# One core, attention then a gated MLP: every engine in written order from the second tile on, with attention's work cut into steps over product slots and the inverse roots folded on partitions

## The chip, the core and the metric

The kernel runs on one core of one Trainium2 chip. The metric is the device time of one execution in microseconds (us), as the median of several runs. The core's engines are TensorE (PE, matmuls), VectorE (DVE), ScalarE (ACT), GpSimd (POOL) and SyncE (SP, which issues most of the DMAs). PE writes its sums to PSUM banks; DVE and ACT read them there.

## The reference

What is computed, cut to what matters:

```python
B, H, S, D = 8, 8, 576, 64                       # q, k, v: fp32
scores = where((rel >= 0) & (rel < 64), q @ k.T / 8, -1e9)   # rel = row - column
attn = exp(scores - max); attn /= sum + 1e-9
x = (attn @ v) as (B*S = 4608 tokens, H*D = 512)
xn = x / sqrt(mean(x*x) + 1e-6) * rms_g
g, val = xn @ w_gate, xn @ w_val                 # 512 x 1536 each
out = (silu(g) * val) @ w_out                    # 1536 x 512
```

## The kernel before

**Tiles.** The 4608 tokens go through the MLP in nine tiles t of 512; the 1536 hidden columns in six chunks c of 256. An fp32 matrix is split in a high and a low half-precision part, and a product is three matmuls (hi·hi, hi·lo, lo·hi; `three`, L799 to L802). Tiles 0 to 2 use ordinary products (`expert_in`: 288 matmuls of 512 columns a tile; gate and value sums `pg`, `pv`). From tile 3 on (`FIRST7 = 3`) `expert_in_7` computes each chunk with seven products in the manner of Strassen: 42 products a tile, each 12 matmuls of 256 columns (L941), in four PSUM banks `bk0`, `bk1`, `bk2`, `bk5`. Between products, ACT copies a bank aside so that it comes free (`snap`, L962: `s1`, `u2`, and `p5`, which lies in `wt11`); DVE adds the copies back (L999, L1002, L1006), and `quad` makes one quarter of a chunk's hidden values: tanh on ACT (L971), two operations on DVE (L972, L973), and for every second one a cast on ACT (L977) and the low part on POOL or, in the last chunk, DVE (L978). `expert_out` then makes the tile's output with 144 matmuls of 512 columns; `store` scales on ACT (L1024, `ot`) and writes by DMA.

**Attention.** Batch b (576 tokens) has four pairs of heads, n = 4b + hp. Batches 0 and 1 are computed up to tile 0 and 1; pairs 8 to 31 beside the MLP, a tile or so ahead of need, in *visits* (`visit`), one every 8 of a tile's 32 half steps. In a visit PE computes the values of pair n − 2 (L511, `xp`) and the scores of pair n (L386, `sc`); then DVE masks and finds minima in nine operations (L399), ACT takes nine exps (L402), DVE finishes the sums (L431, L432); later POOL normalises and moves blocks of 32 rows in sixteen operations (`move`, L371), and DVE transposes 32x32 blocks (`turn`, L374, L375), before visit n + 2. When the fourth pair of a batch has been drained (L573) and squared (L579, L584), `normalise` computes the inverse root mean square: PE sums the squares over partitions and broadcasts them (`tot`, L710), DVE iterates on all 128 partitions (L698, L699, three times L703 to L705: 11 operations, once for each of the two pieces of a batch that fall in two tiles), scales x (L750), and `combine` prepares the seven-product operands (L783 to L796: casts on ACT, low parts on POOL, sums on DVE). In tiles 1 and 2 `prepare` also builds the sums of weights for the seven products (DVE, ACT, DMA) in four steps a chunk.

**What sets the order.** All this is written in one stream: `tick` calls `advance` at half steps, which takes events from a list `plan` sorted by due step. The Tile framework then schedules each engine's queue by its own model of times, within the data's dependences. Only PE is held to the written order, from tile 1, chunk 3 on (`ORDERED = (1, 3)`): `group` issues each group of instructions after PE's last one. DVE, ACT and POOL run their queues in the order that the scheduler gave. An engine takes its queue strictly in order, as the trace shows it: the first instruction that waits holds those behind it.

## Time and profile before

| | us |
|---|---|
| median of 3 runs (1050.73, 1053.23, 1054.05) | 1053.23 |
| the profiled execution | 1047.25 |
| its span, first to last instruction | 1045.5 |
| PE busy | 970.2 |
| DVE busy | 666.3 |
| POOL busy | 529.9 |
| ACT busy | 509.8 |
| mean granted PE clock (1 is full) | 0.974 |

The profile's rows give times from the span's start. In a row of the timeline stand start, duration, engine, line, operation, out<-in and count; in brackets the idle time of the engine ahead of it and the instruction that ended it. In a row of the waits stand who waited for whom, us in total, how often, and the longest. In a row for a stretch of time stand its length, and for each engine the busy time with the number of instructions, then the granted PE clock, the DMA engines' busy share and GB/s.

By the first product of each, the tiles begin at 58.2, 218.9, 337.8, 459.1, 559.5, 664.2, 769.1, 869.6 and 955.7 us, and the last output ends at 1042.0.

### The profile page before, as it was taken

The page shows a single profiled execution, that of the slowest core. Times are in us where ns is not written, and L with a number is a line of the kernel's source. Part 1 is how long each engine was busy: PE and PEld are TensorE (multiplying, and loading weights), DVE is VectorE, ACT ScalarE, POOL GpSimd, SP SyncE. Part 2 cuts the span into 40 slices and gives each one's busy share as a digit, 9 for nine tenths or more (in the row PEclk, how much of TensorE's full clock was granted, in tenths as well). Part 3 has the DMA queues.
Part 4 walks back from the last instruction along what each step waited for, and adds up shares of the span by engine and source line. Part 5 has one row for each costly group of instructions (what it writes and reads, how often), then busy time and mean ns, then how long its engine had stood idle before and what let it go on. Part 6 is the DMA issues. An engine that isn't in the chain of part 4 may idle for free.

```text
span 1045.5 us, 20648 instructions
## 1 busy us (share of the span) xinstructions
PE 970.2 (93%) x7739; PEld 629.6 (60%) x7751; DVE 666.3 (64%) x1725; ACT 509.8 (49%) x1303; POOL 529.9 (51%) x667
## 2 busy tenths in 40 slices
PE   7789987899988799989999899999989999999998
PEld 5444544344444255458846784688568847866875
DVE  5688857447778665856685668666866575531550
ACT  5567877235432444346535663556355524522540
POOL 3425634817856566765765675667566313200210
PEclk9989998999999899999999999999999999999999
DMA  7657963013320554137724672466235514732501
GB/s 284 191 164 218 256 185 92 21 54 117 96 78 26 151 158 146 66 117 232 216 81 148 201 217 85 122 222 219 74 108 176 177 40 141 211 113 78 166 1 41
DMA packets 81316, 143.43 MB, mean 137 GB/s; under 512 B 25792, under 2 KB 38336, under 8 KB 81216
## 3 DMA queue, kind: packets, MB, share of 16 engines
q1 hardware_dynamic: 80640, 140.93, 44.1%
q8 instruction: 61, 1.00, 0.4%
q10 hardware_dynamic: 576, 1.18, 0.3%
q14 instruction: 39, 0.32, 0.1%
HBM read 121.64 MB, written 20.45 MB: 136 GB/s over the span
## 4 chain that ended last, share of the span: by engine, by line
PE 45%; DVE 19%; POOL 18%; ACT 13%; issue 4%; DMA 1%; POOLq 0%; SPq 0%; ACTq 0%; DVEq 0%
POOL pm L371 17%; PE bk L941 16%; ACT pm L402 6%; PE bk L800 3%; PE bk L802 3%; PE bk L801 3%; PE xp L511 3%; DVE xb L750 2%; PE sc L386 2%; DVE pm L374 2%; DVE r L703 2%; PE pg L800 2%; DVE r L704 2%; DVE r L705 2%; PE pg L801 2%
## 5 line engine op out<-in xcount | busy, mean ns | idle before, releaser
L941 PEld LDWEIGHTS <-wt 128*128 128x128 f16 x3024 | 297.5, 99 | 66.4 <-issue 27.6
L371 POOL TENSOR_TENSOR pm<-pm,st 32x288 f32<-32x288 f32 (+1 forms) x384 | 271.6, 707 | 125.2 <-DVE st L432 38.7
L941 PE MATMUL bk<-xn,wt 128*128 128x256 f16 x1728 | 210.3, 274 | 17.4 <-ACT wt L962 7.0
L941 PE MATMUL bk<-wt,wt 128*128 128x256 f16 x1224 | 152.8, 275 | 7.0 <-ACT s L962 7.0
L978 POOL TENSOR_TENSOR h<-th,h 128x512 f16<-128x512 f32 x60 | 69.2, 1158 | 165.7 <-ACT h L977 149.2
L800 PE MATMUL bk<-wt,h 128*128 128x512 f16 (+1 forms) x300 | 111.2, 371 | 0.0
L801 PE MATMUL bk<-wt,h 128*128 128x512 f16 (+1 forms) x300 | 111.1, 370 | 0.0
L802 PE MATMUL bk<-wt,h 128*128 128x512 f16 (+1 forms) x300 | 111.1, 370 | 0.0
L402 ACT ACTIVATE pm<-pm,st 128x128 f32<-128x128 f32 (+1 forms) x216 | 82.1, 381 | 12.8 <-DVE st L399 12.8
L971 ACT ACTIVATE th<-bk,hsc 128x256 f32<-128x256 f32 x108 | 51.1, 473 | 73.1 <-DVE bk L999 37.1
L802 PEld LDWEIGHTS <-h 128*128 128x128 f16 x436 | 42.8, 98 | 53.6 <-issue 5.1
L800 PEld LDWEIGHTS <-h 128*128 128x128 f16 x436 | 43.2, 99 | 49.3 <-issue 3.8
L801 PEld LDWEIGHTS <-h 128*128 128x128 f16 x436 | 42.9, 98 | 47.9 <-issue 2.8
L374 DVE STREAM_TRANSPOSE pm<-pm 128x1024 f32<-128x1024 f32 x24 | 29.8, 1243 | 65.1 <-POOL pm L371 65.1
L972 DVE SCALAR_TENSOR_TENSOR th<-th,bk 128x256 f32<-128x256 f32 x108 | 44.9, 416 | 39.5 <-ACT th L971 39.5
L800 PE MATMUL pg<-xn,wt 128*128 128x512 f16 x144 | 56.8, 394 | 12.0 <-ACT ot L1024 7.9
L386 PE MATMUL sc<-kv,q 64*64 64x128 f32 (+1 forms) x1056 | 57.1, 299 | 8.4 <-DMA q<-q 4.9
L999 DVE TENSOR_TENSOR bk<-bk,s 128x512 f32<-128x512 f32 x36 | 25.1, 696 | 60.7 <-PE bk L941 53.4
L800 PE MATMUL pv<-xn,wt 128*128 128x512 f16 x144 | 56.3, 391 | 7.4 <-DVE th L849 7.3
L801 PEld LDWEIGHTS <-wt 128*128 128x128 f16 x296 | 29.7, 100 | 53.2 <-issue 22.9
L783 ACT CAST xn<-xb 128x192 f16<-128x192 f32 (+7 forms) x33 | 12.9, 423 | 97.1 <-DVE xb L750 97.0
L977 ACT CAST h<-th 128x512 f16<-128x512 f32 x72 | 44.5, 618 | 29.3 <-DVE th L973 29.3
(189 smaller groups left out, 1916.1 us busy)
## 6 DMA issues: line engine op xcount, KB each, us to landing
wt<-sevens SPq DMA_DIRECT2D x108, 512.0 KB, 4.3
kv<-kv SPq DMA_DIRECT2D x28, 608.0 KB, 4.6
wt<-sevens SPq DMA_DIRECT2D x36, 256.0 KB, 3.5
q<-q SPq DMA_DIRECT2D x28, 288.0 KB, 3.6
...
```

Of the source, the lines that this page charges most:

```text
L371: nc.gpsimd.tensor_tensor(m[to, :us, fr], p[fr, :us, to], r, ALU.mult)
L374: nc.vector.transpose(p[:, : NBLK - 1, :], m[:, : NBLK - 1, :])
L386: nc.tensor.matmul(out.rearrange("p (n c) -> p n c", c=D), lhsT=qt[hd, j * D : (j + 1) * D], rhs=halves[hd, :1, :] if j == 0 else halves[h ...
L402: nc.scalar.activation(part, part, AF.Exp, bias=low, scale=-1.0, accum_out=total)
L800: nc.tensor.matmul(acc, lhsT=lh, rhs=rh, start=first, stop=False)
L801: nc.tensor.matmul(acc, lhsT=lh, rhs=rl, start=False, stop=False)
L802: nc.tensor.matmul(acc, lhsT=ll, rhs=rh, start=False, stop=last)
L941: nc.tensor.matmul(acc[:, i * HT : (i + 1) * HT], lhsT=w[:, i, l, kt, :], rhs=b[:, m, kt, :], start=at_start, stop=kt == 1 and j == 2, ski ...
L971: nc.scalar.activation(cols, acc[:, :HT], AF.Tanh, scale=th_scale[:, c : c + 1])
L972: nc.vector.scalar_tensor_tensor(cols, cols, 1.0, acc[:, :HT], ALU.add, ALU.mult)
L977: nc.scalar.copy(hh, th)
L978: (nc.vector if t and c == NC - 1 else nc.gpsimd).tensor_tensor(hl, th, hh, ALU.subtract)
```

## The change

From tile 1, chunk 0 on, `in_written_order` ties each instruction of PE, DVE, ACT and POOL to the one written before it on its engine, so that the scheduler no longer moves any; SP is left free. The code is rewritten so that the written order is meant as it stands. Half steps become halves and fractions; `slot_at` counts in *slots*, one for each product or its like. In a visit, masks are written one to a slot, each exp one slot after its mask, the finish after the last, the sixteen moves one at a time from slot 11.3 on, 0.8 apart, and the transposition as three operations (two of 512 columns for one of 1024, and the rest) from four slots ahead of visit n + 2 on. Tanh and the first gating operation come right after the gate product in tiles 1 and 2; casts and low parts are deferred by one and two slots. Squares come one slot, their sum two slots after the copy.

The inverse roots of a batch (from batch 2 on) are computed once: four matmuls put the sums of 144 tokens each on 32 partitions, the 11 DVE operations work on 144 columns, and `spread` makes five new fp32 matmuls a batch (`rb`) that broadcast the roots to all partitions, from which L750's successor reads them in PSUM. `combine` comes in seven steps without spare tiles for t2 and t4; the low parts of t1, t2 and t4 (six operations a batch) go from POOL to DVE. `prepare` comes in eight steps a chunk.

The core of the diff:

```diff
-ORDERED = (1, 3)
+ORDERED = (1, 0)
+MASK_AT, MASK_BY, WEIGH = 1, 1, 1
+MOVE_AT, MOVE_BY, TURN_AT = 11.3, 0.8, -4
+NORM_AT, NORM_BY, NORM_GAP = 5, 0.75, 2
+RUSH = 12
+GATE, HH_7, HH_8 = 0, 1, 1
...
+    def in_written_order(start, engines):
+        last = {}
+        for k, ins in enumerate(nc.cur_bb.bb.instructions):
+            if ins.engine not in engines:
+                continue
+            if k >= start and ins.engine in last:
+                tc.add_manual_dep(ins, last[ins.engine].name, NO_SYNC, reason="written order")
+            last[ins.engine] = ins
...
+    def turn(p, m, part):
+        if part < 2:
+            js = slice(4 * part, 4 * part + 4)
+            nc.vector.transpose(p[:, js, :], m[:, js, :])
+        else:
+            nc.vector.transpose(p[0:D, NBLK - 1, :], m[0:D, NBLK - 1, :])
...
+        by = MASK_BY if n >= RUSH else 0.5
+        for i, u in enumerate(order):
+            after(MASK_AT + by * i, partial(mask_of, u))
+            after(MASK_AT + by * i + WEIGH, partial(weight_of, u))
+        after(MASK_AT + by * NBLK + WEIGH, finish)
...
+            s0 = slot_at(visit_at(NPAIR * b + 5))
+            for k, part in enumerate(normalise_all(b, norm)):
+                at_slot(s0 + NORM_AT + NORM_BY * k + (NORM_GAP if k > 2 else 0), part)
...
-                for k in range(4):
-                    events.append((i0 + (MOVES[hp] + 0.8 * k if n > 11 else 3.5 + 0.4 * k), partial(moved, hp, k)))
-                events.append((visit_at(n + 2) - half_steps * (b - 1) - 3, partial(turned, hp)))
+                s0 = slot_at(visit_at(n))
+                for k in range(16):
+                    when = MOVE_AT + MOVE_BY * k if n >= RUSH else MOVE_AT - 4 + 0.5 * k
+                    at_slot(s0 + when, partial(moved, hp, k // 4, k % 4))
+                for k in range(3):
+                    at_slot(slot_at(visit_at(n + 2)) + TURN_AT - 2 * (n < 16) + k, partial(turned, hp, k))
...
-    def roots_of_all(b, ssq, a, z):
-        tot = x_bank(f"tot_{b}_{a}")[:, : z - a]
-        nc.tensor.matmul(tot, lhsT=ones, rhs=ssq[:, a:z], start=True, stop=True)
+    def roots_folded(b, norm):
+        m, r, w = (norm["ssq"][:, S // 4 * i : S // 4 * (i + 1)] for i in range(3))
+        norm["r"] = r
+        def totals():
+            tot = x_bank(f"tot_{b}")[:, : S // 4]
+            for i in range(4):
+                nc.tensor.matmul(
+                    tot[32 * i : 32 * i + 32, :],
+                    lhsT=one.to_broadcast([P, 32]),
+                    rhs=norm["ssq"][:, S // 4 * i : S // 4 * (i + 1)],
...
+    def spread(b, r, a, z):
+        rb = x_bank(f"rb_{b}_{a}")
+        n = S // 4
+        for i in range(a // n, (z + n - 1) // n):
+            lo, hi = max(a, i * n), min(z, i * n + n)
+            nc.tensor.matmul(
+                rb[:, lo - a : hi - a],
+                lhsT=first_of[:, i : i + 1].to_broadcast([P, P]),
+                rhs=r[:, lo - i * n : hi - i * n],
...
+            parts("t1", x12, nc.vector)
...
+            parts("t2", x12, nc.vector)
...
+            parts("t4", x21, nc.vector)
...
+                if name == "g":
+                    th = wk.tile([P, TT], F32, tag="t2k", name=f"th_{t}_{f}", bufs=T2K)
+                    nc.scalar.activation(th, a, AF.Tanh, scale=th_scale[:, c : c + 1])
+                    nc.vector.scalar_tensor_tensor(th, th, 1.0, a, ALU.add, ALU.mult)
...
+            defer(HH_8, partial(hi_copy, hh, th))
+            defer(HH_8 + 1, partial((nc.vector if t and c == NC - 1 else nc.gpsimd).tensor_tensor, hl, th, hh, ALU.subtract))
...
-    for j in range(4 * NC):
-        at_step(PREP0 + (PREP1 - PREP0) * j / (4 * NC), partial(prepare, j // 4, j % 4))
+    for j in range(8 * NC + 1):
+        at_slot(s0 + (s1 - s0) * j / (8 * NC), partial(prepare, j // 8, j % 8))
...
+    in_written_order(written, [e.engine for e in (nc.tensor, nc.vector, nc.scalar, nc.gpsimd)])
```

Three places show what moves. The line numbers of the changed kernel differ: L415 is the exp (L402), L1156 the copy of a bank (L962), L1167 the tanh (L971), L1219 the output copy (L1024), L981 the cast or low part of h in tiles 1 and 2 and of the quads (L977, L978).

The first is ACT's queue at the start of tile 4, at the visit of pair 22. `pm` and `st` are that pair's weights and sums, `s` and `wt_92` the two copies of banks, `ot_3` the last output of tile 3. Before:

```order
L402 ACTIVATE pm_5810,st_5811<-pm_5810,st_5811 128x64
L402 ACTIVATE pm_5810,st_5811<-pm_5810,st_5811 128x128 x8
L1024 ACTIVATE ot_3_5850<-bk_4565,hsc 128x512
L962 COPY s_4571<-bk_4564 128x512
L962 COPY wt_92<-bk_4567 128x512
L971 ACTIVATE th_0_0_5907<-bk_4566,hsc 128x256
L962 COPY u_4572<-bk_4564 128x512
L971 ACTIVATE th_0_0_5907<-bk_4567,hsc 128x256
```

In the changed kernel:

```order
L1219 ACTIVATE ot_3_5821<-bk_4545,hsc 128x512
L415 ACTIVATE pm_5805,st_5806<-pm_5805,st_5806 128x64
L1156 COPY s_4551<-bk_4544 128x512
L415 ACTIVATE pm_5805,st_5806<-pm_5805,st_5806 128x128
L1156 COPY wt_92<-bk_4547 128x512
L415 ACTIVATE pm_5805,st_5806<-pm_5805,st_5806 128x128
L1167 ACTIVATE th_0_0_5876<-bk_4546,hsc 128x256
L415 ACTIVATE pm_5805,st_5806<-pm_5805,st_5806 128x128
L1156 COPY u_4552<-bk_4544 128x512
L415 ACTIVATE pm_5805,st_5806<-pm_5805,st_5806 128x128
L1167 ACTIVATE th_0_0_5876<-bk_4547,hsc 128x256
```

The output copy now stands ahead of the exps, and the copies of banks and the tanhs stand one by one between exps.

The second is DVE's queue in tile 4 around the transposition of the same pair (`pm_5810` before, `pm_5805` after; L1197, L1200 and L1204 are the additions L999, L1002 and L1006, L1176 and L1177 the gating L972 and L973, L412 the mask, L386 and L388 the transposition). Before, in the first chunks of the tile:

```order
L1002 TENSOR_TENSOR bk_4567<-bk_4567,u_4572 128x512
L972 SCALAR_TENSOR_TENSOR th_0_0_5907<-th_0_0_5907,bk_4567 128x256
L973 SCALAR_TENSOR_TENSOR th_0_0_5907<-bk_4567,th_0_0_5907 128x256
L1006 TENSOR_TENSOR wt_92<-bk_4564,wt_92 128x512
L374 STREAM_TRANSPOSE pm_5810<-pm_5810 128x1024
L999 TENSOR_TENSOR bk_4566<-bk_4566,s_4571 128x512
L972 SCALAR_TENSOR_TENSOR th_0_1_5969<-th_0_1_5969,wt_92 128x256
L375 STREAM_TRANSPOSE pm_5810<-pm_5810 64x128
L973 SCALAR_TENSOR_TENSOR th_0_1_5969<-wt_92,th_0_1_5969 128x256
L972 SCALAR_TENSOR_TENSOR th_1_0_5996<-th_1_0_5996,bk_4566 128x256
```

In the changed kernel, among chunks 2 and 3:

```order
L1197 TENSOR_TENSOR bk_4546<-bk_4546,s_4551 128x512
L1176 SCALAR_TENSOR_TENSOR th_3_0_6280<-th_3_0_6280,bk_4546 128x256
L1177 SCALAR_TENSOR_TENSOR th_3_0_6280<-bk_4546,th_3_0_6280 128x256
L412 ISA pm_6099,st_6100<-sc_1_6080,blocked 128x128
L412 ISA st_6100 128x1
L386 STREAM_TRANSPOSE pm_5805<-pm_5805 128x512
L1176 SCALAR_TENSOR_TENSOR th_2_1_6258<-th_2_1_6258,bk_4544 128x256
L1177 SCALAR_TENSOR_TENSOR th_2_1_6258<-bk_4544,th_2_1_6258 128x256
L448 TENSOR_SCALAR st_6100<-st_6100 128x9
L449 RECIPROCAL st_6100<-st_6100 128x9
L386 STREAM_TRANSPOSE pm_5805<-pm_5805 128x512
L388 STREAM_TRANSPOSE pm_5805<-pm_5805 64x128
```

The transposition has moved from the first chunk after its visit to the third and fourth, near the end of the next pair's masks, and stands in three parts.

The third is DVE's queue at the end of tile 4, at the roots of batch 5 (`ssq`, `xb`: its squares and values). Before, the first of the two pieces:

```order
L699 TENSOR_SCALAR r_5_0_6824<-r_5_0_6823 128x192
L703 TENSOR_TENSOR r_5_0_6825<-r_5_0_6824 128x192
L704 SCALAR_TENSOR_TENSOR r_5_0_6825<-r_5_0_6825,r_5_0_6823 128x192
L705 SCALAR_TENSOR_TENSOR r_5_0_6824<-r_5_0_6825,r_5_0_6824 128x192
L703 TENSOR_TENSOR r_5_0_6825<-r_5_0_6824 128x192
L704 SCALAR_TENSOR_TENSOR r_5_0_6825<-r_5_0_6825,r_5_0_6823 128x192
L705 SCALAR_TENSOR_TENSOR r_5_0_6824<-r_5_0_6825,r_5_0_6824 128x192
L703 TENSOR_TENSOR r_5_0_6825<-r_5_0_6824 128x192
L704 SCALAR_TENSOR_TENSOR r_5_0_6825<-r_5_0_6825,r_5_0_6823 128x192
L705 SCALAR_TENSOR_TENSOR r_5_0_6824<-r_5_0_6825,r_5_0_6824 128x192
L750 SCALAR_TENSOR_TENSOR xb_5805<-xb_5805,gsb,r_5_0_6824 128x192 x4
```

In the changed kernel, for the whole batch (L774 reads the sums, L811 is the iteration, L900 the scaling, L412 a mask of pair 25):

```order
L774 TENSOR_SCALAR ssq_5802<-tot_6807 128x144
L811 TENSOR_SCALAR ssq_5802<-ssq_5802 128x144
L811 TENSOR_TENSOR ssq_5802<-ssq_5802 128x144
L811 SCALAR_TENSOR_TENSOR ssq_5802<-ssq_5802 128x144 x2
L811 TENSOR_TENSOR ssq_5802<-ssq_5802 128x144
L811 SCALAR_TENSOR_TENSOR ssq_5802<-ssq_5802 128x144 x2
L412 ISA pm_6735,st_6736<-sc_1_6716,blocked 128x128
L412 ISA st_6736 128x1
L811 TENSOR_TENSOR ssq_5802<-ssq_5802 128x144
L811 SCALAR_TENSOR_TENSOR ssq_5802<-ssq_5802 128x144 x2
L412 ISA pm_6735,st_6736<-sc_1_6716,blocked 128x128
L412 ISA st_6736 128x1
```

The 11 operations stand once, on 144 columns, with masks of the next pair among them; the scaling follows behind two more masks and reads `rb`, which PE makes from the roots.

More of the change, by code (lines that the diff above doesn't have):

```diff
@@ L5 @@
 import math
-from contextlib import ExitStack, contextmanager
+from contextlib import ExitStack
+from fractions import Fraction
 from functools import partial
@@ L78, in tile_window_attention_moe @@
     banks = {}
-    in_order = {"on": False}
-    @contextmanager
-    def group():
-        if not in_order["on"]:
-            yield
-            return
-        last = next(x for x in reversed(nc.cur_bb.bb.instructions) if x.engine == nc.tensor.engine)
-        with tc.issue_after(last):
-            yield
+    NO_SYNC = mybir.DependencyInfo(mybir.DependencyClass.NoSync, mybir.DependencyReason.DATA)
+    def in_written_order(start, engines):
[6 more added lines that the diff above has]
+            last[ins.engine] = ins
     def x_bank(name):
@@ L627, in visit @@
     def visit(n):
+        here["slot"] = slot_at(visit_at(n))
         before = visits.get(n - 2)
@@ new lines, in run @@
+    def run(parts):
+        for part in parts:
+            part()
+    def spread(b, r, a, z):
[7 more added lines that the diff above has]
+                rhs=r[:, lo - i * n : hi - i * n],
+                start=True,
+                stop=True,
+                skip_group_check=True,
+            )
+        return rb
@@ new lines, in normalise_all, with __init__, parts, root @@
+    def normalise_all(b, norm):
+        return LazyParts(b, norm).parts()
+    class LazyParts:
+        def __init__(self, b, norm):
+            self.b, self.norm, self.made = b, norm, {}
+        def parts(self):
+            out = [partial(self.root, k) for k in range(3)]
+            for piece in range(2):
+                t = place_of(self.b, piece)[2]
+                out += [partial(self.scaled, piece, k) for k in range(2)]
+                out += [partial(self.part, piece, k) for k in range(7 if t >= FIRST7 else 2)]
+            return out
+        def root(self, k):
+            if k == 0:
+                self.roots = roots_folded(self.b, self.norm)
+            self.roots[k]()
+        def scaled(self, piece, half):
+            a, z, t, o = place_of(self.b, piece)
+            if half == 0:
+                self.made[piece] = spread(self.b, self.norm["r"], a, z)
+            for kt in (2 * half, 2 * half + 1):
+                x = self.norm["x"][:, kt, a:z]
@@ L804, in tile_window_attention_moe, with defer, tick @@
     hs = {}
-    steps = {"now": 0}
-    def tick():
+    steps = {"now": Fraction(0)}
+    waiting = []
+    strict = {"on": False}
+    def defer(ticks, part):
+        if strict["on"]:
+            waiting.append([ticks, part])
+        else:
+            part()
+    def tick(d):
+        steps["now"] += d
+        due = [w for w in waiting if w[0] <= 0]
+        waiting[:] = [[k - 1, part] for k, part in waiting if k > 0]
+        for _, part in due:
+            part()
         advance(steps["now"])
-        steps["now"] += 1
     def h_tile(t, c):
```

341 lines of the change are left out of this document (206 added, 135 removed).

## The prediction

> **What bounds the kernel now.** I read the page's busy shares first, then the busy time tile by tile, then TensorE's waits, then the timeline around the longest of them.
>
> ```profile
> PE 970.2 (93%) x7739; PEld 629.6 (60%) x7751; DVE 666.3 (64%) x1725; ACT 509.8 (49%) x1303; POOL 529.9 (51%) x667
> ```
>
> PE is the bound as an average. The nine tiles (the last, 955.70 to 1042.00, has no attention and is left out here) show where it isn't:
>
> ```profile
> core 0: us, PE busy (x) PEld busy (x) DVE busy (x) ACT busy (x) POOL busy (x), PEclk, DMA share, GB/s
> 58.20:218.90 160.70, 145.36 (x932) 74.72 (x941) 110.51 (x300) 103.28 (x222) 85.59 (x101) 0.93 0.50 149
> 218.90:337.80 118.90, 109.91 (x772) 53.33 (x771) 90.04 (x206) 48.19 (x136) 72.19 (x86) 0.99 0.26 76
> 337.80:459.10 121.30, 109.37 (x724) 52.49 (x724) 82.68 (x208) 53.32 (x160) 74.89 (x92) 0.96 0.43 129
> 459.10:559.50 100.40, 99.02 (x941) 73.19 (x941) 70.76 (x175) 49.61 (x134) 67.64 (x89) 0.98 0.50 152
> 559.50:664.20 104.70, 97.92 (x942) 72.51 (x941) 73.22 (x195) 54.76 (x157) 67.51 (x90) 1.00 0.52 162
> 664.20:769.10 104.90, 99.46 (x942) 73.18 (x941) 73.96 (x195) 54.71 (x157) 67.37 (x91) 0.98 0.50 159
> 769.10:869.60 100.50, 94.76 (x798) 69.21 (x797) 61.70 (x151) 48.98 (x122) 49.26 (x61) 0.98 0.45 134
> 869.60:955.70 86.10, 86.10 (x650) 63.42 (x649) 32.99 (x68) 31.69 (x58) 12.29 (x11) 1.00 0.48 143
> ```
>
> Tile 7 (869.60) carries no attention, and PE is busy for all of its 86.10 us: nothing can be won there. In tiles 1 to 6 PE is idle for 8.99, 11.93, 1.38, 6.78, 5.44 and 5.74 us (length less PE busy), together 40.3. Who is waited for:
>
> ```profile
> PE pg L800 <- ACT ot L1024: 7.9, 2, 4.5
> PE pv L800 <- DVE th L849: 7.3, 6, 3.1
> PE bk L941 <- ACT wt L962: 7.0, 3, 3.4
> PE bk L941 <- ACT s L962: 7.0, 3, 2.7
> PE bk L941 <- DVE th L973: 5.3, 4, 1.3
> PE bk L941 <- ACT ot L1024: 5.1, 1, 5.1
> PE po L801 <- DVE wt L236: 3.8, 1, 3.8
> ```
>
> These are few and long, and none is an engine out of capacity: DVE, the busiest beside PE, works 73.22 of 104.70 us in tile 4. They are short operations behind long ones. The start of tile 4 shows two such places:
>
> ```profile
> 564.06 0.39 ACT L402 ACTIVATE pm<-pm,st 128x128 f32<-128x128 f32 x1
> 564.44 0.66 ACT L1024 ACTIVATE ot<-bk,hsc 128x512 f32<-128x512 f32 x1
> 565.01 0.56 ACT L962 COPY s<-bk 128x512 f32<-128x512 f32 x1
> 565.63 1.47 PE L941 MATMUL bk<-wt,wt 128*128 128x256 f16 x12 [2.04 <-ACT s L962]
> 565.13 11.09 POOL L371 TENSOR_TENSOR pm<-pm,st 32x288 f32<-32x288 f32 x16 [4.18 <-ACT ot L1024]
> 576.26 1.24 DVE L374 STREAM_TRANSPOSE pm<-pm 128x1024 f32<-128x1024 f32 x1 [4.50 <-POOL pm L371]
> 579.04 0.59 ACT L962 COPY wt<-bk 128x512 f32<-128x512 f32 x1 [0.43 <-DVE th L973]
> 579.67 2.56 PE L941 MATMUL bk<-xn,wt 128*128 128x256 f16 x22 [3.41 <-ACT wt L962]
> ```
>
> First, the copy that frees bank 0 (L962, 565.01) stands behind the last of nine exps and an output copy, and PE waits 2.04. Second, the transposition waits 4.50 at the head of DVE's queue for POOL's sixteen moves (11.09 us), the gating of finished products stands behind it, and PE loses 3.41. The L973 rows of the waits are the same wait once more.
>
> The gaps also cost clock:
>
> ```profile
> 775.84 2.44 PE L941 MATMUL bk<-wt,wt 128*128 128x256 f16 x12 [2.67 <-ACT s L962]
> 776.20:779.60 3.40, 3.40 (x19) 2.42 (x17) 1.17 (x3) 1.14 (x3) 3.17 (x5) 0.50 0.87 236
> 565.00:570.00 5.00, 4.37 (x41) 3.92 (x41) 2.49 (x5) 2.79 (x7) 4.50 (x7) 1.00 0.90 277
> sum 24.00, PE 21.87 PEld 11.09 DVE 14.31 ACT 9.91 POOL 18.52; mean PE 3.65 PEld 1.85 DVE 2.39 ACT 1.65 POOL 3.09
> ```
>
> After the wait of 2.67 the granted clock is 0.50 for 3.4 us; after the 2.04 at 565 it stays 1.00. The last row adds up the six stretches at half clock from tile 1 on: PE works 21.87 us there, of which half, 10.9, is lost. The Trainium skill, "TensorE: Matmul & The Clock Gate", in "HAM oscillation — how this bites in real kernels", gives the rule as no idle gap over about 3.4 us. The trace is stricter: 2.67 was enough. By the page's rule my 2 us for left-over half clock below would be 0.
>
> **The change part by part.** All against the profiled execution, 1047.25 us.
>
> *Fixed order, steps spread over slots.* A slot is one product, 1.31 us: tile 7's 86.10 less its 144 output matmuls of 0.2156 (worked out below), over 42 products. Exps go one to a slot between the snaps, and the output copy goes ahead of them. The moves go singly from 11.3 slots after their visit, the transposition in three parts from 24 slots on, at 31.4 us. The moves take 11.09 and so end after 14.8 + 11.09 = 25.9 us, or 30.5 if four of POOL's roundings stand between them:
>
> ```profile
> L978 POOL TENSOR_TENSOR h<-th,h 128x512 f16<-128x512 f32 x60 | 69.2, 1158 | 165.7 <-ACT h L977 149.2
> ```
>
> If all of it works, idle and half clock from tile 1 on go: −40.3 − 10.9 = −51.2. What takes their place:
>
> - Tiles 1 and 2: DVE carries 90.04 and 82.68 us in tiles that would last about 108, and now waits in order for each tanh with masks, transpositions and weight preparation behind it. Between none and all of the present 20.9 us; I take a third, +7, since the load leaves DVE a fifth of the time to catch up in.
> - The start of tile 3 needs new banks and so the last output copy (0.66 plus handing over): +1 of the 5.1.
> - Tiles 3 to 6: DVE waits inside each gating:
>
> ```profile
> 565.61 0.70 DVE L999 TENSOR_TENSOR bk<-bk,s 128x512 f32<-128x512 f32 x1 [0.62 <-ACT s L962]
> 567.31 0.42 DVE L973 SCALAR_TENSOR_TENSOR th<-bk,th 128x256 f32<-128x256 f32 x1
> ```
>
> From 565.61 to 567.73 is 2.12 us for one of the four of a chunk; the one without the addition takes 2.12 − 0.70 = 1.42. A chunk is 3 × 2.12 + 1.42 = 7.8 of its 7 × 1.31 = 9.2 us, a tile 6 × 7.8 = 46.7, and attention adds 73.22 − 32.99 = 40.2: 86.9 of some 98. It fits, with little room. Bounds: 0, and the 19.3 idle there now; nearer the low end, since tile 7 runs the same gating with no wait: +4.
> - Left-over half clock: +2, between 0 and 10.9.
>
> *Roots folded.* Before, each batch computes them twice at full width; now once on 144 columns, then TensorE spreads them (rb).
>
> ```profile
> 560.60 0.28 DVE L399 CUSTOM_DVE_ANT_0 pm<-sc,blocked 128x128 f32<-128x128 f32 x1
> 331.50 0.36 DVE L704 SCALAR_TENSOR_TENSOR r<-r,r 128x192 f32<-128x192 f32 x1
> 638.45 0.71 DVE L704 SCALAR_TENSOR_TENSOR r<-r,r 128x192 f32<-128x192 f32 x1
> 634.92 11.78 POOL L371 TENSOR_TENSOR pm<-pm,st 32x288 f32<-32x288 f32 x16 [7.26 <-DVE st L432]
> 633.42 0.49 PE L710 MATMUL tot<-ssq,one 128*128 128x192 f32 x2
> 633.75 0.38 PE L800 MATMUL bk<-wt,h 128*128 128x512 f16 x1
> 641.51 0.81 PE L710 MATMUL tot<-ssq,one 128*128 128x384 f32 x2
> ```
>
> On PE 192 columns of a batch's sums take 633.75 − 633.42 = 0.33, so its 576 columns 0.98 us. The four narrow ones cost as much if they run one after another, a quarter if side by side; rb streams the same 576 columns, another 0.98. Six batches: +1 to +7 with issue, I take +4.
> DVE's operations fall from 22 to 11, which at 0.39 to 0.75 each leaves it 4 to 8 us a batch, off the path. But rb is a wait on PE's own queue: 24 output products stand between sums and rb (between 633.75 and 641.51 there are 36, so 0.2156 each, 5.2 us), and all that follows on PE stands behind rb. Alone, eleven operations 0.39 apart (0.36 and some 0.03 between, the trace's spacing; its 192 columns are more than 144) take 4.3 at most; at the 0.71 that the same form takes while POOL's moves run (638.45, inside the moves of 634.92), with the same 0.04 between them, 8.2; one mask of the next pair, 0.28, stands among them. So each batch waits between 0 (4.6, less than 5.2) and 3.3 (8.5 − 5.2). The moves of the pair before should be done as the roots begin (25.9 against 24.9 us after that pair's visit: the next visit is 14 slots on and the roots 5 more), so +0.7 each, +4.
> The Trainium skill, "SBUF — State Buffer", in "SBUF: two separate sides", says that a DVE operation with two SBUF inputs and a GpSimd operation exclude each other for a whole instruction. The 0.71 against 0.36 agrees, and so do the moves, 11.78 here for 11.09 at 565; it speaks against putting PE behind this chain.
>
> *Moved roundings.* Six low parts a batch go from POOL to DVE, which hides them in what it won on the roots: 0; if DVE is full they are part of rival A. Casts and low parts of h come one and two slots later; the outputs need those of chunk 5 last, behind 30 output matmuls of chunks 0 to 4 (6.5 us), which cover two slots of 1.31: 0. Squares and their sum come one and two slots later, and nothing waits for them but the roots: 0. The weights' preparation, in eight steps for four, has the same operations and DMAs; the DMAs on SP's queue come later by a step, ahead of loads that tile 3 needs a tile later: 0, and if that cover goes, the first product of tile 3 waits for its load. Two transpositions of half the size for one cost DVE the same columns: 0.
>
> *Tile 0* keeps the scheduler; only its plan is cut finer. Its 3.8 us wait for L236 may go or come twice: −3.8 to +3.8, I take −2.
>
> Sum: 1047.25 − 51.2 + 7 + 1 + 4 + 2 + 4 + 4 − 2 = 1016. The profiled execution lies 6.0 below the median of 1053.23 and 3.5 below the fastest of the runs; I add 4: **1020**, own range 1010 to 1030.
>
> **Rivals.**
> - *D, nearly all is won.* Roots never wait, tiles 1 and 2 lose 2, tiles 3 to 6 nothing: 13 less, 1007. Tile 7's flawless 86.10 speaks for it, DVE's 86.9 of 98 against.
> - *C, the waits stay.* Moves later than 31.4 us (the margin is 0.9 to 5.5) keep the transposition waiting in front of the gatings: L962's 7.0 on wt, L973's 5.3, and some 5 of half clock: +17, 1037.
> - *A, DVE saturates.* Each of the 24 chunks of tiles 3 to 6 loses 0.5 to 1.3 us, 12 to 31 in all: 1032 to 1051, middle 1041.
> - *E, the shared port.* By the exclusion told above as the trace shows it, moves still run when roots begin, and each of six batches waits 3.3 instead of 0.7: +16, 1036. The rule is that of the "SBUF — State Buffer" page of the Trainium skill.
> - *B, slower.* One mechanism: in fixed order a mask, transposition or root step ahead of a gating delays the bank that PE needs two products later, in every chunk. Before, the scheduler chose what goes first; now a step that isn't ready holds all behind it. It decides from 1.6 us a chunk on: 24 × 1.6 = 38, to 1058. A whole gating, 2.12, gives 24 × 2.12 = 51: 1071. For it: the 7.8 of 9.2. Against: DVE is idle 31 us of tile 4, so each delay must be repaid within a chunk.
>
> **How the numbers follow.** Likeliest 0.47, D 0.15, C 0.11, A 0.10, E 0.08, B 0.09. About 0.3% (3.2 us) is what can be told from no change. Faster (under 1050): all but B and a sliver of A and B's edge: 0.87; same 0.03; slower 0.10. The range 1003 to 1045 leaves out B, D's lower quarter and A's upper third, 0.09 + 0.04 + 0.04 = 0.17.
>
> **What would show it.** Right: no row of PE waiting for "s", "wt" or "ot" above 1 us in tiles 4 to 6; tiles 4 and 5 at 99 to 101 us; the half-clock stretches after 400 us gone; the transposition not waiting on POOL. Roots: PE waiting for ssq before rb under 1 us a batch (E: about 3). Tile 1 near 112. Wrong: PE waits of about a microsecond in every chunk, with DVE (A, B) as releaser, or DVE still idle for POOL in front of a transposition (C).

## The result, and the profile after

The changed kernel takes 1038.05 us (median of 4 runs, 1035.82 to 1040.11), the one before 1052.68 in the same comparison: a ratio of 0.9862 (95% interval 0.9835 to 0.9889). It is faster, by 14.6 us or 1.4%, clear of the noise; the forecast was 1020, 33 us faster. 1038 lies inside the wide range of 1003 to 1045, outside the narrow one of 1010 to 1030, and less than half of the gain came. The profiled execution takes 1038.57 us, its span 1036.8, against 1047.25 and 1045.5.

The tiles of the changed kernel, 0 to 6, with the columns of the same view of before (length; busy time of PE, weight loads, DVE, ACT, POOL; PE clock; DMA share; GB/s):

```profile
59.30:223.60 164.30, 149.21 (x915) 75.29 (x914) 108.07 (x275) 100.25 (x205) 73.01 (x85) 0.90 0.48 143
223.60:346.80 123.20, 111.13 (x813) 55.17 (x812) 96.36 (x239) 54.35 (x159) 85.15 (x100) 0.97 0.29 86
346.80:453.10 106.30, 105.37 (x739) 52.00 (x738) 67.91 (x184) 48.79 (x136) 69.39 (x84) 1.00 0.44 135
453.10:557.20 104.10, 99.73 (x954) 73.01 (x954) 71.12 (x194) 53.70 (x155) 64.88 (x84) 1.00 0.52 160
557.20:661.20 104.00, 99.72 (x956) 73.08 (x955) 71.33 (x194) 54.38 (x156) 64.47 (x84) 1.00 0.52 164
661.20:764.70 103.50, 99.71 (x956) 73.07 (x955) 69.78 (x194) 54.17 (x156) 64.86 (x84) 1.00 0.51 160
764.70:859.60 94.90, 93.74 (x811) 69.03 (x810) 59.28 (x142) 45.83 (x117) 41.23 (x52) 1.00 0.43 130
```

Tile 2 lost 15 us and is nearly without idle time (106.30, PE busy 105.37). Tile 6 lost 5.6. But tile 0 is 3.6 longer than before, tile 1 4.3 longer, tile 3 3.7 longer, and tiles 4 and 5 gained 0.7 and 1.4. What PE waits for in the changed kernel:

```profile
PE pv L960 <- DVE th L1025: 6.1, 2, 4.9
PE bk L1136 <- DVE th L1177: 5.3, 11, 0.6
PE bk L1136 <- ACT wt L1156: 4.9, 11, 1.2
PE rb L818 <- DVE ssq L811: 3.8, 4, 2.3
PE xp L534 <- DVE pm L388: 2.7, 4, 1.6
PE bk L1136 <- ACT ot L1219: 0.8, 1, 0.8
```

The output copy went from 13.0 us in both forms to 0.8, the copy `s` from 7.0 to nothing. In their place stand waits in two shapes: one of 4.9 in tile 1, and 22 of about half a microsecond in tiles 3 to 6.

The long one, in tile 1 (timeline rows of POOL, DVE and PE):

```profile
269.54 2.62 POOL L381 TENSOR_TENSOR pm<-pm,st 32x256 f32<-32x256 f32 x4
272.19 0.71 DVE L386 STREAM_TRANSPOSE pm<-pm 128x512 f32<-128x512 f32 x1 [7.07 <-POOL pm L381]
273.96 0.58 PE L960 MATMUL pv<-xn,wt 128*128 128x512 f16 x1 [4.87 <-DVE th L1025]
```

The transposition stands in DVE's fixed order 7.07 us for POOL's last moves, the gating behind it, and PE 4.87 with it, in the very way that the change removed from tiles 4 to 6.

One of the short ones, in tile 4 (PE, POOL, DVE, ACT, PE):

```profile
604.75 1.47 PE L1136 MATMUL bk<-wt,wt 128*128 128x256 f16 x12
602.90 1.45 POOL L614 TENSOR_TENSOR ssq<-ssq,kv 128x576 f32<-128x576 f32 x1
602.28 0.81 DVE L1176 SCALAR_TENSOR_TENSOR th<-th,wt 128x256 f32<-128x256 f32 x1 [0.57 <-ACT th L1167]
603.13 1.51 DVE L1177 SCALAR_TENSOR_TENSOR th<-wt,th 128x256 f32<-128x256 f32 x1
606.19 0.57 ACT L1156 COPY wt<-bk 128x512 f32<-128x512 f32 x1
606.81 1.47 PE L1136 MATMUL bk<-xn,wt 128*128 128x256 f16 x12 [0.59 <-ACT wt L1156]
```

L1177 takes 0.42 us where one input is in a bank. Here both, `wt` and `th`, are in SBUF, and it takes 1.51: it ends 0.29 after POOL's sum of 1.45 does. The next addition, tanh and copy follow in order, and PE waits. Of the 24 such gatings in tiles 3 to 6 eleven take 1.26 or 1.51, and there are eleven PE waits for the copy of `wt` and eleven for L1177.

The idle time is not the whole price. The two products start at 604.75 and 606.81, 2.06 apart, where a product without a wait takes 1.31: the wait costs 0.75, and the column has 0.59, because the end of the last matmul reaches 0.16 into it. By this estimate the 22 waits, 10.2 us in the rows above, cost 10.2 + 22 × 0.16 = 13.7.

### The profile page after: what moved, and what is told of

Read it like the earlier page. It is cut to its first block, busy times and chain, and to the rows that moved or that the text cites. A ratio compares the mean times of both kernels' runs of the same rounds, so it can differ in the third digit from the quotient of the medians.

```text
span 1036.8 us, 20838 instructions
## 1 busy us (share of the span) xinstructions
PE 975.6 (94%) x7835; PEld 633.0 (61%) x7835; DVE 649.9 (63%) x1721; ACT 507.4 (49%) x1303; POOL 507.8 (49%) x634
## 4 chain that ended last, share of the span: by engine, by line
PE 46%; DVE 18%; ACT 7%; issue 3%; POOL 2%; DMA 0%; DVEq 0%; ACTq 0%; POOLq 0%
PE bk L1136 18%; PE bk L960 5%; PE bk L962 5%; PE bk L961 5%; DVE th L1176 3%; PE xp L534 3%; ACT th L1167 3%; DVE th L1177 3%; PE sc L399 2%; DVE pm L412 2%; DVE ssq L811 2%; ACT pm L415 2%; POOL pm L381 1%; DVE bk L1197 1%; PE po L960 1%
## 5 line engine op out<-in xcount | busy, mean ns | idle before, releaser
L381 POOL TENSOR_TENSOR pm<-pm,st 32x288 f32<-32x288 f32 (+1 forms) x384 | 279.5, 728 | 100.6 <-DVE st L449 46.6
L1136 PE MATMUL bk<-xn,wt 128*128 128x256 f16 x1728 | 209.2, 272 | 11.5 <-DVE th L1177 5.3
L981 POOL TENSOR_TENSOR h<-th,h 128x512 f16<-128x512 f32 x78 | 91.7, 1175 | 191.5 <-ACT h L981 177.6
L1136 PE MATMUL bk<-wt,wt 128*128 128x256 f16 x1224 | 150.4, 273 | 0.3 <-ACT u L1156 0.3
L962 PE MATMUL bk<-wt,h 128*128 128x512 f16 (+1 forms) x300 | 111.1, 370 | 0.0
L415 ACT ACTIVATE pm<-pm,st 128x128 f32<-128x128 f32 (+1 forms) x216 | 83.9, 389 | 50.3 <-DVE st L412 49.8
L1167 ACT ACTIVATE th<-bk,hsc 128x256 f32<-128x256 f32 x108 | 51.0, 472 | 99.5 <-DVE bk L1197 66.8
L1176 DVE SCALAR_TENSOR_TENSOR th<-th,bk 128x256 f32<-128x256 f32 x108 | 45.2, 418 | 54.6 <-ACT th L1167 54.2
L981 ACT CAST h<-th 128x512 f16<-128x512 f32 x94 | 57.7, 614 | 35.5 <-DVE th L1026 21.7
L962 PEld LDWEIGHTS <-h 128*128 128x128 f16 x436 | 42.9, 98 | 52.5 <-issue 4.4
L960 PE MATMUL pv<-xn,wt 128*128 128x512 f16 x144 | 56.6, 393 | 8.2 <-DVE th L1025 6.1
L1197 DVE TENSOR_TENSOR bk<-bk,s 128x512 f32<-128x512 f32 x36 | 24.9, 692 | 57.3 <-PE bk L1136 57.3
L961 PE MATMUL pv<-xn,wt 128*128 128x512 f16 x144 | 56.1, 390 | 0.0
L962 PE MATMUL pv<-xn,wt 128*128 128x512 f16 x144 | 55.8, 388 | 0.0
```

Source lines behind the costliest of these rows:

```text
L381: nc.gpsimd.tensor_tensor(m[to, :us, fr], p[fr, :us, to], r, ALU.mult)
L415: nc.scalar.activation(part, part, AF.Exp, bias=low, scale=-1.0, accum_out=total)
L960: nc.tensor.matmul(acc, lhsT=lh, rhs=rh, start=first, stop=False)
L961: nc.tensor.matmul(acc, lhsT=lh, rhs=rl, start=False, stop=False)
L962: nc.tensor.matmul(acc, lhsT=ll, rhs=rh, start=False, stop=last)
L981: part()
```

## The experiments

Each ratio is to the kernel before, measured beside it; the changed kernel's is 0.9862 (0.9835 to 0.9889).

**1. Is it the written order, or the split?** Only PE is tied:

```diff
-    in_written_order(written, [e.engine for e in (nc.tensor, nc.vector, nc.scalar, nc.gpsimd)])
+    in_written_order(written, [e.engine for e in (nc.tensor,)])
```

> The changed code, but only TensorE is tied to the written order; the scheduler orders VectorE, ScalarE and GpSimd as it did before the change. If the written order on those three brings the gain: the scheduler again puts exps, transpositions and gatings where its model has them, the waits of 2 to 5 us come back, and the time is 1045 to 1060. If the splitting of the code and the folded roots bring it: 1036 to 1042, as the changed kernel.

1060.41 us, ratio 1.0067 (1.0052 to 1.0081): the order on the other engines is worth about 22 us, and without it the change is a loss. The mechanism is another than expected. Its waits of PE:

```profile
PE rb L818 <- DVE ssq L811: 21.4, 5, 8.8
```

and the roots' operations in this kernel, then in the changed one (minimum, median and maximum in ns):

```profile
L811 DVE SCALAR_TENSOR_TENSOR ssq<-ssq x36: 307/683/715, 318.3 to 856.8; 128x144 f32<-128x144 f32 x36
```

```profile
L811 DVE SCALAR_TENSOR_TENSOR ssq<-ssq x36: 295/308/641, 315.9 to 836.1; 128x144 f32<-128x144 f32 x36
```

Under the scheduler the roots run beside POOL's moves and take 683 ns each, and PE, which now stands behind them at rb, waits. For the same batch (its roots begin at 645.29 here and at 630.64 in the changed kernel), first with only PE tied:

```profile
643.35 11.52 POOL L381 TENSOR_TENSOR pm<-pm,st 32x288 f32<-32x288 f32 x16 [7.26 <-DVE st L449]
652.50 0.64 PE L818 MATMUL rb<-ssq,first_of 128*128 128x144 f32 x4 [3.59 <-DVE ssq L811]
```

and then in the changed kernel:

```profile
623.97 9.49 POOL L381 TENSOR_TENSOR pm<-pm,st 32x288 f32<-32x288 f32 x12
632.31 1.31 DVE L811 SCALAR_TENSOR_TENSOR ssq<-ssq 128x144 f32<-128x144 f32 x2
634.00 0.65 DVE L811 SCALAR_TENSOR_TENSOR ssq<-ssq 128x144 f32<-128x144 f32 x2
635.91 0.64 PE L818 MATMUL rb<-ssq,first_of 128*128 128x144 f32 x4 [0.55 <-DVE ssq L811]
```

With only PE tied the moves cover the whole chain, and three batches wait 3.6 us each: rival E. The longest wait, 8.8 at batch 2, is only partly that, because the scheduler also put four steps of the weights' preparation, 5.0 us, inside that chain. In written order the moves are not done either when the roots begin; they end 2.8 us later (633.46), so the first operations take twice as long and the rest 0.3 each, and PE waits 0.55. The median of 308 hides this.

**2. Roots as before, in written order.** The folded chain is dropped, and `scaled` takes its factor from `roots_of_all` of the kernel before, once for each piece:

```diff
-                self.made[piece] = spread(self.b, self.norm["r"], a, z)
+                self.made[piece] = roots_of_all(self.b, self.norm["ssq"], a, z)
```

> The changed kernel, with the inverse roots as before the change: 128 partitions, all columns, once for each piece, scaled from SBUF, no broadcast on TensorE; all in written order at the places where the folded ones stood. If folding pays by what it takes off VectorE: 11 more and wider operations a batch (0.4 to 1.0 us) hold the gatings and masks behind them, and the time rises by 5 to 15 us, to 1043 to 1053. If the wait for rb on TensorE is dearer than the work it saves: the waits of 3.8 us and some 4 us of new matmuls go and the time falls by 3 to 7 us, to about 1033.

1095.77 us, ratio 1.0413 (1.0386 to 1.0440), worse than either theory:

```profile
PE xp L534 <- DVE pm L388: 52.0, 6, 15.5
```

Two chains of 11 wide operations stand ahead of the next transposition in DVE's order, and PE waits for that 9 to 15 us a batch. The chains do not stand quite where the folded one stood: the edit starts them where `spread` was, 4.25 slots behind the first step of the folded roots, so part of the price may be that they start late. At these places the order needs the folding; other places for the unfolded roots were not tried.

**3. The broadcast one slot later.**

```diff
-NORM_AT, NORM_BY, NORM_GAP = 5, 0.75, 2
+NORM_AT, NORM_BY, NORM_GAP = 5, 0.75, 3
```

> The broadcast of the roots (rb) and what follows it stand one slot (1.31 us) later; the roots stay. If rb's waits on TensorE, 3.8 us over four batches with 2.26 in the first, are the path: they fall to about 1 (the first keeps about 1), and the time by 2 to 3 us, to about 1035.5. If what follows rb is the path (the operands of the next tile): the wait turns up at the next tile's first products, and the time stays at 1038 or rises.

1034.28 us, ratio 0.9816 (0.9799 to 0.9832): 4 us, more than the 2 to 3 expected and, within the noise, the 3.8 us of waits. The waits at rb are gone but one of 0.96, and so is one of 0.69 at the visit behind it in tile 4.

**4. The shared port in tiles 3 to 6.** POOL's low parts of h and its sums of squares are cut in quarters:

```diff
+    def in_quarters(eng, out, a, b, op):
+        if eng is not nc.gpsimd:
+            eng.tensor_tensor(out, a, b, op)
+            return
+        n = out.shape[-1] // 4
+        for i in range(4):
+            cs = slice(i * n, (i + 1) * n)
+            eng.tensor_tensor(out[:, cs], a[:, cs], b[:, cs], op)
```

> GpSimd's low parts of h in tiles 3 to 8 (1.16 us) and its sums of squares from batch 2 on (1.40 us) are each cut into four operations of a quarter of the columns. Port theory (a GpSimd operation holds VectorE's two-input gating of the third quarter, th with wt, for its whole length, which is what makes TensorE wait in tiles 3 to 6): the longest L1177 falls from 1.5 to about 0.8 us, TensorE's waits for the copy of wt and for L1177, 10.2 us together, to 5 or less, and the time by 3 to 6 us, to about 1033. Rival (the waits come from the written order, from masks, transpositions and exps ahead of the gating): GpSimd only gets more to issue, the gaps stay, and the time stays at 1038 or rises by 1 to 2.

1031.55 us, ratio 0.9800 (0.9784 to 0.9815). The second gating operation in the changed kernel, with one input in a bank and then with both in SBUF, and the latter here:

```profile
L1177 DVE SCALAR_TENSOR_TENSOR th<-bk,th x108: 423/424/426, 459.0 to 1004.0; 128x256 f32<-128x256 f32 x108
L1177 DVE SCALAR_TENSOR_TENSOR th<-wt,th x36: 424/426/1509, 465.3 to 1002.6; 128x256 f32<-128x256 f32 x36
```

```profile
L1186 DVE SCALAR_TENSOR_TENSOR th<-wt,th x36: 424/533/775, 465.6 to 998.4; 128x256 f32<-128x256 f32 x36
```

With one input in a bank none of 108 is longer than 426 ns, though 24 of the 57 in tiles 3 to 5 lie wholly inside POOL's work; with both in SBUF the longest fell from 1509 to 775. Tiles 3 to 5, with POOL busy for longer than before:

```profile
454.50:556.10 101.60, 99.25 (x957) 73.11 (x955) 66.91 (x194) 53.66 (x154) 71.01 (x120) 1.00 0.53 165
556.10:657.50 101.40, 99.22 (x956) 73.09 (x955) 68.07 (x194) 54.51 (x157) 70.83 (x120) 1.00 0.53 167
657.50:758.50 101.00, 99.29 (x956) 73.08 (x955) 67.00 (x194) 54.30 (x157) 71.09 (x120) 1.00 0.52 164
```

2.5 us a tile; tile 6 gave 2.4 back, with a wait of 1.8 for a transposition and 3 us at half clock behind it. PE's waits for the copy of `wt` are gone and those for this gating are 1.5 of 5.3. The order is the same, so the length of POOL's operations beside a gating with both inputs in SBUF is shown to be the cause of this part.

**5. Both together.** 

> The two edits that made it faster together: GpSimd's low parts and sums in four operations, and the broadcast of the roots a slot later. They act at different places (the gating in the chunks; the wait for rb in the outputs), so their gains of some 6.5 and 4 us against the changed kernel should add: about 1028, tiles 3 to 5 at about 100. If they share a cause (VectorE late in the outputs because of GpSimd), the sum is less: 1030 to 1032.

1028.17 us, ratio 0.9773 (0.9749 to 0.9797). They add: tiles 4 and 5 take 99.6 and 99.7.

**6. Tile 1: order or work?** First the transposition of pairs 8 to 11 three slots later, behind the next pair's finish:

```diff
-                    at_slot(slot_at(visit_at(n + 2)) + TURN_AT - 2 * (n < 16) + k, partial(turned, hp, k))
+                    at_slot(slot_at(visit_at(n + 2)) + (TURN_AT + 1 if n < RUSH else TURN_AT - 2 * (n < 16)) + k, partial(turned, hp, k))
```

> Only the place of the transpositions of pairs 8 to 11 changes: from six slots ahead of the visit that needs them to three, so that they stand behind the next pair's finish on VectorE instead of ahead of it. Convoy theory (VectorE waits for GpSimd's moves with the next pair's masks and finish behind it, which starts GpSimd's next moves late, so the next transposition waits longer): the waits of the transposition for moves in tile 1, 2.55 and 7.07 us, fall below 2 in all, TensorE's 4.87 us gap and the half clock behind it go, tile 1 falls from 123.2 to about 116, and the time by 6 to 8 us, to about 1031. Rival (GpSimd is simply over capacity there: 11.2 us of moves, 1.4 of sums and 2.5 low parts of 1.16 in the 13.1 us between visits): the wait moves to the visit, where TensorE waits for the transposition, and the time stays within 2 us of 1038.

1041.61 us, ratio 0.9894 (0.9877 to 0.9910). DVE's waits for moves fall from 11.5 to 1.9, but PE waits instead, and tile 1 grows to 129.5:

```profile
PE xp L534 <- DVE pm L388: 14.5, 8, 4.7
```

The convoy theory falls: the wait moved to the visit, as the rival has it. Then the low parts of h in tile 1 on DVE:

```diff
-            defer(HH_8 + 1, partial((nc.vector if t and c == NC - 1 else nc.gpsimd).tensor_tensor, hl, th, hh, ALU.subtract))
+            defer(HH_8 + 1, partial((nc.vector if t == 1 or t and c == NC - 1 else nc.gpsimd).tensor_tensor, hl, th, hh, ALU.subtract))
```

> The changed kernel, with the low parts of h in tile 1 (ten operations of 1.16 us on GpSimd) on VectorE instead. If GpSimd over capacity is what costs tile 1 its gaps (15 us of work for 13.1 us between visits, as the later transposition already suggests): GpSimd's moves end earlier, the transposition's waits of 2.55 and 7.07 us fall below 4 together, TensorE's 4.87 us gap and the half clock behind it go, and the time falls by 5 to 7 us, to about 1032. Rival (VectorE, 96 of 123 us busy there, is as full as GpSimd): its gatings come later by the added 0.7 to 1.2 us each, tile 1 stays near 123 and the time near 1038.

1038.54 us, ratio 0.9868 (0.9846 to 0.9890): tile 1 at 122.9, no gain, as the rival has it: DVE's waits for moves fall from 11.5 to 6.4, and others come. Then the preparation of weights later (`PREP0, PREP1 = 40, 86`):

> The changed kernel, with the weights' preparation spread from half step 40 to 86 instead of 32.2 to 80: some 9 us of VectorE's work leaves tile 1 (96 of 123 us busy) for tile 2 (68 of 106). If VectorE's load, and its operations beside GpSimd's, delay masks, finishes and so GpSimd's moves in tile 1: the transposition's waits of 2.55 and 7.07 us and TensorE's 4.87 us gap shrink to half, rb's wait of 2.26 goes, tile 1 falls to 117 to 119 and the time by 4 to 6, to about 1033. If GpSimd's capacity alone sets it: the gaps stay, time 1036 to 1039.

1039.42 us, ratio 0.9883 (0.9862 to 0.9905): tile 1 121.5, tile 2 110.8; moved, not saved. Both together:

> The changed kernel with the preparation later, and the low parts of h in tile 1 on VectorE. The low parts alone did not shorten the time: the waits for GpSimd fell from 11.5 to 6.4 us, but new ones came. If tile 1 is held by both engines at once, taking work from both gives what neither gives alone: transposition's waits under 3 us, tile 1 at 113 to 116, time about 1030. If VectorE's load alone counts, it is worse than the preparation alone by 1 to 3 us.

1042.35 us, ratio 0.9900 (0.9873 to 0.9926): not 1030, and 2.9 above the preparation alone, which is inside the noise. Tile 1:

```profile
223.70:347.00 123.30, 112.21 (x812) 56.18 (x811) 95.49 (x238) 53.10 (x156) 71.80 (x90) 0.97 0.27 80
```

POOL has 13 us less to do than in the changed kernel, no transposition in tile 1 waits for it any more, and the tile is as long. So POOL's moves of pairs 8 to 11 themselves are shortened. This kernel leaves out five of their nine blocks of columns and serves for its time alone.

```diff
+        us = us if n >= RUSH else 4
```

> The changed kernel, with GpSimd's sixteen moves of pairs 8 to 11 on four of the nine blocks of columns only (the other blocks are not normalised or moved; the transpositions keep their size and read the first four again). GpSimd's work in tile 1 falls by some 5.5 us a visit, VectorE's stays. If GpSimd's work sets tile 1: the transposition no longer waits, TensorE's gaps of 4.87, 2.26 and 1.64 us and the half clock go, tile 1 falls from 123 to 112 to 115 and the time by 8 to 10 us, to about 1029. If the written order on VectorE sets it: tile 1 stays above 120, the time above 1035.

1027.62 us, ratio 0.9779 (0.9755 to 0.9804). Tile 1:

```profile
220.70:333.20 112.50, 108.21 (x814) 54.06 (x811) 91.87 (x237) 54.50 (x159) 72.85 (x100) 1.00 0.32 94
```

10.7 us less in the same order: the moves set tile 1. It is not POOL's busy time as such, which is 72.85 here and was 71.80 in the run before. Whether it is that the moves of a pair end sooner, or that each shuts DVE out for a shorter time (DVE is busy 91.87 for 96.36 with the same operations), is not settled. Nor is POOL far over capacity: the expectations count some 15 us of POOL's work for 13.1 us between visits, but where nothing waits the visits stand at least 15.5 apart (219.6, 235.1 and 252.0 here).

**7. Tile 0.** First the kernel before, once more:

> The kernel before once more, for its trace. The profiled execution of before was 5.4 us below the median of its runs. If tile 0 differs between executions of the same program by how its stretches at half clock fall: tile 0 lasts 163 to 166 us here, as in the traces of the changed kernel (162 to 166 in five), and the execution takes about 1052. If the change itself lengthens tile 0: it lasts 160 to 161 again.

```profile
58.50:220.20 161.70, 146.41 (x942) 75.18 (x942) 111.18 (x301) 103.78 (x223) 86.36 (x102) 0.94 0.49 147
```

161.70, and 160.70 in the first trace; the changed kernel has 164.30, and 161 to 166 in the ten other traces in which tile 0 is written as the change has it. So the change lengthens tile 0 by up to 5 us, though none of its engines is tied there. With tile 0 written as before:

```diff
-                tick(0.5)
+                tick(0.5 if t else 1)
...
-                if name == "g":
+                if name == ("g" if t else "v"):
```

> The changed kernel, with tile 0 written as before the change (whole half steps, tanh after both products); from tile 1 on nothing differs. Tile 0 lasted 162 to 166 us in seven traces of the changed code and 160.8 and 161.7 in two of before, with 31 us at half clock for 20. If the finer plan, by the scheduler's other order in tile 0, costs this: tile 0 falls to about 161 and the time by 3 to 5 us, to about 1034. If the difference lies in the start or in what tile 1 takes over (its first visit): tile 0 gets shorter and tile 1 longer by as much, time 1037 to 1039.

1024.95 us, ratio 0.9745 (0.9723 to 0.9767), 13 us for a few lines, 12 of them in tile 0:

```profile
58.20:210.50 152.30, 141.99 (x916) 72.29 (x915) 104.60 (x275) 100.43 (x205) 75.69 (x85) 0.95 0.51 155
```

Tile 0 is not 161 but 152: the rest of the change shortens it by some 9. The two halves apart, the finer steps undone first:

> The changed kernel with whole half steps again in tile 0, tanh still right after the gate product there. If it is the finer steps, which issue half of tile 0's pieces in the middle of a product, that made the scheduler's order worse: tile 0 falls to 152 as with both undone, time 1025. If it is tanh: tile 0 stays at 162 to 166, time 1036 to 1039.

1033.18 us, ratio 0.9836 (0.9811 to 0.9862), between the two expectations and not told apart from the changed kernel:

```profile
58.70:219.40 160.70, 146.43 (x908) 75.17 (x916) 106.78 (x276) 100.05 (x206) 73.64 (x86) 0.92 0.49 146
```

> The changed kernel with tanh after both products in tile 0 only, the finer steps kept. The counterpart: if the place of tanh made tile 0 slower, tile 0 falls to about 152 and the time to about 1025; if the finer steps did, tile 0 stays at 162 to 166 and the time at 1036 to 1039; if both share, about 1031 here and there.

1027.78 us, ratio 0.9785 (0.9763 to 0.9806):

```profile
59.00:213.00 154.00, 142.55 (x908) 72.48 (x916) 105.26 (x276) 100.76 (x206) 75.58 (x86) 0.96 0.51 153
```

Tanh ahead of the value product, where the scheduler still orders ACT and DVE, costs most of it: 8 us of tile 0 with whole half steps (160.7 for 152.3), 10 with the finer ones (164.3 for 154.0). The finer steps cost 2 to 4. Part of the price is clock: the stretches at half clock in tile 0 add up to 20.5 us in the kernel before and 30.6 in the changed one,

```profile
sum 20.50, PE 17.04 PEld 8.98 DVE 16.45 ACT 14.84 POOL 16.50; mean PE 4.26 PEld 2.24 DVE 4.11 ACT 3.71 POOL 4.13
```

```profile
sum 30.60, PE 24.78 PEld 12.35 DVE 23.49 ACT 18.07 POOL 18.20; mean PE 6.19 PEld 3.09 DVE 5.87 ACT 4.52 POOL 4.55
```

in which PE lost half of 17.0 and of 24.8, so 3.9 more in the changed kernel, about as much as the tile grew. Which operation the early tanh held up was not settled.

**8. What they add up to.** Quarters, broadcast, tile 0 and preparation:

> All edits that should help, together: GpSimd's operations in quarters, rb a slot later, tile 0 as before, preparation later. From 1028 of the first two: 1020 if tile 0 (4) and the preparation (4 to 5) add up; 1024 if only one of them does; 1028 if neither.

1018.61 us, ratio 0.9680 (0.9659 to 0.9702). It is near the 1020, but by other terms: tile 0 gives some 12 and not 4, and the preparation nothing, as the next run shows. With the preparation where the change put it:

> GpSimd's operations in quarters, rb a slot later, tile 0 as before; the preparation where the change put it, since moving it alone gained nothing in tiles 1 and 2 (232.3 us for 229.6). 1028 less the 13 of tile 0: 1015; tiles 1 and 2 at 230 together. If the later preparation had helped among these edits: 1019 or more.

1017.01 us, ratio 0.9678 (0.9656 to 0.9701): the same. Tiles 3 to 6 take 395.1, and tile 1 is as long as ever:

```profile
212.90:337.60 124.70, 112.13 (x813) 55.58 (x811) 97.07 (x239) 54.37 (x159) 86.41 (x106) 0.97 0.30 89
```

Two attempts at tile 1 on top of that, with moves of pairs 8 to 11 on DVE:

```diff
-            nc.gpsimd.tensor_tensor(m[to, :us, fr], p[fr, :us, to], r, ALU.mult)
+            (nc.vector if n < RUSH and qq % 2 else nc.gpsimd).tensor_tensor(m[to, :us, fr], p[fr, :us, to], r, ALU.mult)
```

> The fastest so far (1017) with eight of the sixteen moves of pairs 8 to 11 on VectorE. GpSimd's work a visit falls by 5.5 us as with the moves halved, where tile 1 fell to 112.5; VectorE takes eight more operations of about 0.4 us a visit. If VectorE has the room (its waits for GpSimd's moves go, 11 us in tile 1): tile 1 falls from 124.7 to about 115, the time to about 1008. If its moves wait for GpSimd's (two inputs in SBUF on both engines) and hold the gatings: tile 1 stays above 120 and the time at 1014 or more.

1023.14 us, ratio 0.9747 (0.9723 to 0.9770). Tile 1, and the moves on DVE:

```profile
217.70:342.80 125.10, 110.97 (x813) 54.42 (x812) 110.04 (x258) 54.80 (x159) 69.94 (x82) 0.99 0.29 85
```

```profile
L381 DVE TENSOR_TENSOR pm<-pm,st x32: 416/588/1926, 173.0 to 289.0; 32x288 f32<-32x288 f32 x16, 32x256 f32<-32x256 f32 x16
```

Against the kernel without this edit POOL has 16.5 us less to do in tile 1 (69.94 for 86.41), DVE 13.0 more (110.04 for 97.07), and the tile is no shorter: a move that can take 416 ns on DVE takes 588 in the median and up to 1926. Most of the 6 us that the time rose are in tile 0, 159.2 for 153.6, where pair 8 is already moved and the scheduler still orders DVE. With a quarter of the moves (`qq == 3`):

> The same with four of sixteen moves on VectorE: 2.8 us a visit off GpSimd, which brings its 15.4 us a visit under the 13.1 between visits. If capacity is the threshold: most of the gain, tile 1 at 116 to 118, time about 1010. If each move on VectorE only waits in GpSimd's place: 1016 to 1019.

1016.21 us, ratio 0.9673 (0.9652 to 0.9694), the same as without. Tile 1:

```profile
214.40:335.60 121.20, 109.53 (x813) 54.04 (x812) 103.36 (x246) 54.62 (x159) 79.18 (x94) 1.00 0.30 87
```

It is 3.5 shorter, which the time does not show beyond the noise. So half of the moves handed from POOL to DVE gained nothing in tile 1, a quarter little; only taking work out of the moves gained 10.

## Why the prediction was right or wrong

By its own steps, the forecast on the profiled execution's scale was 1016 and the measurement 1038.6. Spread over the tiles, the terms gave tiles 3 to 6 396.9 us (410.5 − 19.3 idle − 4.8 of half clock + 1 + 4 + four batches of 0.7 for waits and 0.7 for matmuls), tiles 1 and 2 222.9, tile 0 158.7. Measured: 406.5, 229.5 and 164.3, which is 9.6 + 6.6 + 5.6 = 21.8 of the 22.5 missing.

- **Right: the waits it named are gone.** Copies of banks no longer wait behind nine exps; from tile 3 on transpositions wait 0.3 us for POOL in all. Of the sizes, the start of tile 3 (1, measured 0.8), the matmuls of the roots (0.7 a batch; in tile 3 the sums and rb take 1.71 for the 0.98 of before) and the left-over half clock (2; one stretch in tile 1, 272.2 to 279.0, where PE lost half of 5.0) fit. The signs that hung on tiles did not come: tiles 4 and 5 take 104.0 and 103.5 for 99 to 101, tile 1 123.2 for about 112.
- **Wrong, "tile 0 keeps the scheduler; only its plan is cut finer … I take −2".** The premise is wrong: in the diff the condition for the early tanh is `name == "g"` alone, so tanh moves in tile 0 too, though the text on the change speaks of tiles 1 and 2. The term had the wrong sign, +3.6 for −2: in that tile tanh's place costs 8 to 10 us and the finer steps 2 to 4, and the rest of the change wins 9. The row taken for the bounds, one wait of 3.8, bounds nothing in a stage in which the whole order may change.
- **Wrong, "tiles 3 to 6 … +4".** The term measures 13.7 by the estimate above (10.2 of it listed as idle time), 9.7 more than forecast, and 9.6 are missing there. The budget of DVE (86.9 of 98) counted each operation at its undisturbed length. The exclusion told at the roots, 0.71 for 0.36, was applied only there; it acts on gatings with both inputs in SBUF, up to 1.51 for 0.42, in about half of the chunks. Tile 7, taken as the sign that the gating runs without a wait, has little of POOL's work beside it (12 us busy). Of the rivals, A had about the size (its low end, 12 us) but not the cause: DVE is busy no more than 71 of 104 us. The Trainium skill, "SBUF — State Buffer", in "SBUF: two separate sides", has the rule, that whichever of the two starts first holds the shared port for its whole instruction and the other waits. The row of 1.51, which ends 0.29 after POOL's 1.45, and the quarters (1509 to 775 ns) agree with it.
- **Wrong, "tiles 1 and 2 … I take a third, +7".** 13.0 us stayed idle, nearly all in tile 1. The argument went by DVE's load alone, and POOL's moves, on which DVE's order waits there, were not in it. The run with shortened moves shows that they set the tile; by which of the ways named there stays open.
- **Rival C happened in tile 1** (waits of 2.55 and 7.07). The moves' distance was worked out with the numbers of later pairs: moves from slot 11.3 on and 0.8 apart hold from pair 12 on. In the diff pairs 8 to 11 have 7.3 and 0.5, and the transposition of pairs 8 to 15 stands six slots ahead of its visit, not four.
- **Rival E's condition held, at a small price; the size of the roots' waits is partly luck.** The forecast had the moves end 1.0 us after the roots begin (25.9 to 24.9); in tiles 3 to 5 they end 2.8 to 3.7 after. Only the first half of the chain meets them, and a batch waits 0.5 us instead of 3.3. The sum of +4 for six batches came out as 3.8 in four, 2.3 of it in the first alone. With the scheduler's order the whole chain meets them, and rb waits 21.4.

With the mis-sized causes taken away or shortened (quarters, broadcast, tile 0 written as before) the kernel takes 1017, where 1020 had been forecast. Tiles 3 to 6 then agree, 395.1 for 396.9; but tile 1 is still some 12 us longer than the 112 named, and the 9 that tile 0 won were not in the forecast, so the agreement of the whole is in part chance.
